# The opening of a gated attention-and-MLP kernel: x halves on two queues, transposes between the first products

## The chip, the cores and the metric

The kernel runs on one core of a Trainium2 chip. Its engines are PE (TensorE, matrix products), DVE (VectorE), ACT (ScalarE), POOL (GpSimd) and SP (SyncE, which here only issues transfers). The metric is the device time of one execution in microseconds. Before the change eight runs gave a median of 148.9 us, from 148.52 to 150.5.

## What is computed

```python
def reference(A_x, A_wqkv, A_w_phi, A_wo, B_x, B_w1, B_w2, gate_w):
    x = A_x                                          # [1, 2048, 512], bf16
    g = sigmoid((x * gate_w).sum(-1, keepdims=True))
    a = A(x, A_wqkv, A_w_phi, A_wo)    # linear attention, 32 heads of 16, softmax feature maps
    b = relu(x @ B_w1) @ B_w2          # 512 -> 1376 -> 512
    return g * a + (1 - g) * b
```

The part that matters here is the start of `b` on the first 512 rows of x, the first x chunk: hidden units are `relu(x @ B_w1)`. The gate's row of 512 weights is put beside `B_w1` as one more column, so that a later product yields the gate's sums as well.

## The kernel before

x is worked on in four chunks of 512 rows. A product on PE contracts over 128 partitions, so x is needed transposed: `XT` holds four feature blocks t of 128 features, each with all rows. Chunks 1 to 3 are transposed by transfers (L172). Chunk 0 is loaded plainly into `XS`, in two halves of 256 rows (L149, events `x00` and `x01`), and transposed by 16 matmuls against an identity (L213, recorded at L217) into PSUM, from where DVE (L227) and ACT (L230) copy it to `XT`.

The order of work is written out by hand. Each engine has a list of operations in program order; an operation names the events that it waits for, and the program turns these into semaphore waits. `free[bank]` names the event after which a PSUM bank may be written again.

The opening goes so:

- ACT's queue issues the load of the gate row (L157). SP's queue issues in this order: the two halves of x (L150), W1 rows of block 0 as a piece of 512 columns and the rest (events `w10a`, `w10`), W1 of blocks 1, 2, 3 (`w11`, `w12`, `w13`; all recorded at L154), then small weights (L164), WV (L166), and the transposed loads (L169, L172).
- PE runs five dummy products (`warm`, L209), the transpose of the gate row (`gatecol`, L203), one dummy product, and 14 of the 16 transposes in four groups. The copies out of PSUM are given to DVE and ACT in turns.
- Then come the slabs (L497). The first eight hidden blocks u of chunk 0 have one PSUM bank each, and slab t adds the product of W1's block (t, u) with `XT` block t into bank u. So a slab is eight products of 512 columns, and four slabs finish eight hidden blocks. Slab 0 is split: four products, the last two transposes, four products. Slabs 1 to 3 follow without a break.
- DVE then does 13 memsets of constants (L519, L521, L524; the last are five, into `EB`), and DVE and ACT apply the ReLU to the eight banks in turns (L241, L239).
- After the slabs PE goes on with two more hidden blocks (`hunit`, L250, recorded at L253), a V tile (`vtile`, L382), projections of the query and key weights (`pre`, L287, eight groups over four banks, copied out by DVE at L292 and ACT at L294), the rest of the hidden columns with the gate column (`rest`, L265), and then the main loop over 16 row tiles.

The banks of the slabs in the order of u are given by:

```python
UB = (3, 4, 5, 0, 6, 7, 2, 1)
```

Of the kernel before, what the change touches and what calls it, by code (L numbers as in the profile page):

```python
# [5 lines left out]
ACT = mybir.ActivationFunctionType  # L6
# [3 lines left out]
BF16 = mybir.dt.bfloat16  # L10
# [47 lines left out]
def bass_gated_mix__linear_kernel_hedgehog__dense_activation_relu__prompt_kernel(  # L58
# [17 lines left out]
    P = 128  # L76
    NT = S // P
    NDT = D // P
# [15 lines left out]
    with ExitStack() as es:  # L94
        E = es.enter_context
        XT = E(nc.sbuf_tensor("XT", [P, NDT, S], BF16))
# [17 lines left out]
        IDN = E(nc.sbuf_tensor("IDN", [P, P], BF16))  # L114
# [4 lines left out]
        GR = E(nc.sbuf_tensor("GR", [NDT, P], BF16))  # L119
# [9 lines left out]
        PS = E(nc.psum_tensor("PS", [P, 8, 512], FP32))  # L129

        XS = OT[:, 0, :].rearrange("p (j d) -> p j d", j=4)
# [7 lines left out]
        p = _Plan(["sp", "pool", "act", "dve", "pe"])  # L139
        free = {b: [] for b in range(8)}  # L140


        xq = x2[0:512, :].rearrange("(p j) d -> p j d", j=4)
# [3 lines left out]
            return oq[:, m, :] if m < 4 else o2[m * P:(m + 1) * P, :]  # L147

        def loadx0(h):  # L149
            p.dma("sp", lambda e: e.dma_start(out=XS[:, 2 * h:2 * h + 2, :], in_=xq[:, 2 * h:2 * h + 2, :]),  # L150
                  f"x0{h}", ev=f"x0{h}")

        def loadw1(t, c0=0, c1=DFF, tag=""):
            p.dma("sp", lambda e: e.dma_start(  # L154
                out=W1[:, t, c0:c1], in_=B_w1[t * P:(t + 1) * P, c0:c1]), f"w1{t}{tag}", ev=f"w1{t}{tag}")

        p.dma("act", lambda e: e.dma_start(out=GR[:, :], in_=gate_w.rearrange("(j p) -> j p", p=P)), "gr", ev="gr")  # L157
        for h in range(2):
            loadx0(h)
        loadw1(0, 0, 4 * P, "a")  # L160
        loadw1(0, 4 * P)
        for t in range(1, NDT):
            loadw1(t)
        p.dma("sp", lambda e: e.dma_start(  # L164
            out=WPS[:, :, :], in_=A_w_phi.rearrange("(g hl) r c -> (hl r) g c", g=NDT)), "wps", ev="wps")
        p.dma("sp", lambda e: e.dma_start(  # L166
            out=WV[:, :, :], in_=A_wqkv[:, 2 * D:3 * D].rearrange("(j p) n -> p j n", p=P)), "wv", ev="wv")
        for i in range(2):
            p.dma("sp", lambda e, i=i: e.dma_start_transpose(  # L169
                out=WQKT[:, 4 * i:4 * i + 4, :], in_=A_wqkv[:, i * D:(i + 1) * D]), f"wqk{i}", ev=f"wqk{i}")  # L170
        for c in range(1, NCH):
            p.dma("sp", lambda e, c=c: e.dma_start_transpose(  # L172
                out=XT[:, :, c * 512:(c + 1) * 512], in_=x2[c * 512:(c + 1) * 512, :]), f"x{c}", ev=f"x{c}")
# [9 lines left out]
            after=["wps"], ev="wd")  # L183
        for gt in range(NDT):
# [4 lines left out]
                after=["wd", "m8"], ev=f"wbd{gt}")  # L189

        p.op("dve", lambda e: e.tensor_tensor(IDN[:, :], ROWI[:, :], COLI[:, :], ALU.is_equal),
             after=["iota0"], ev="idn")
        p.op("dve", lambda e: e.tensor_single_scalar(ROW8[:, :], ROW8[:, :], 4, ALU.arith_shift_right),
             after=["iota"], ev="r8")
# [2 lines left out]
        p.op("dve", lambda e: e.tensor_tensor(M32[:, :], ROW64[:, :], COL16[:, :], ALU.is_equal),  # L197
             after=["r64"], ev="m32")

        def xready(c):  # L200
            return ["xa0", "xa1", "xa2", "xb0", "xb1", "xb3"] if c == 0 else [f"x{c}"]

        def gatecol(bank):  # L203
            gp = PS[:, bank, :].bitcast(BF16)[:, 0:NDT]
            p.op("pe", lambda e: e.transpose(gp, GR[:, :], IDN[0:NDT, 0:NDT]), after=["gr", "idn"], ev="gp")
            p.op("dve", lambda e: e.tensor_copy(W1[:, :, DFF:DFF + 1], gp.unsqueeze(2)), after=["gp"], ev="gw")
            free[bank] = ["gw"]

        def warm(n, cols=512):  # L209
            for _ in range(n):  # L210
                p.op("pe", lambda e: e.matmul(PS[:, 4, 0:cols], ones[:, 0:P], ones[:, 0:cols], start=True, stop=True))

        def xtr(nm, h, dts, bank, evacs):  # L213
            n = 2 * len(dts)
            for i in range(n):
                dt, j = dts[i // 2], 2 * h + i % 2
                p.op("pe", lambda e, i=i, dt=dt, j=j: e.matmul(  # L217
                    PS[:, bank, i * P:(i + 1) * P], XS[:, j, dt * P:(dt + 1) * P], IDN[:, :],
                    start=True, stop=True),
                    after=["idn", f"x0{h}"] + (free[bank] if i == 0 else []), ev=(f"xt{nm}" if i == n - 1 else None))  # L220
            src = PS[:, bank, 0:n * P].rearrange("p (t c) -> p t c", c=256)
            for eng, i0, i1, ev in evacs:
                d = XT[:, dts[i0]:dts[i0] + i1 - i0, h * 256:(h + 1) * 256]
                s = src[:, i0:i1, :]
                if eng == "dve":
                    yield lambda d=d, s=s, ev=ev: p.op(
                        "dve", lambda e: e.tensor_copy(d, s), after=[f"xt{nm}"], ev=ev)  # L227
                else:
                    yield lambda d=d, s=s, ev=ev: p.op(
                        "act", lambda e: e.activation(d, s, ACT.Copy), after=[f"xt{nm}"], ev=ev)  # L230
            free[bank] = [evacs[-1][3]]

        w1all = ["w10a"] + [f"w1{t}" for t in range(NDT)]

# [15 lines left out]
        def hunit(c, kt, eng="act", bank=None):  # L250
            bank = nextbank() if bank is None else bank
            for t in range(NDT):
                p.op("pe", lambda e, t=t: e.matmul(  # L253
                    PS[:, bank, :], W1[:, t, kt * P:(kt + 1) * P], XT[:, t, c * 512:(c + 1) * 512],
                    start=(t == 0), stop=(t == NDT - 1)),
                    after=(xready(c) + w1all + free[bank] if t == 0 else ()),
                    ev=(f"h{c}_{kt}" if t == NDT - 1 else None))
            relu(c, kt, bank, eng)

        def rest(c):  # L260
            bank = nextbank()
            for i in range(4):
                for s in range(NDT):
                    t0 = c * 512 + i * P
                    p.op("pe", lambda e, i=i, s=s, t0=t0: e.matmul(  # L265
                        PS[:, bank, i * P:i * P + NR + 1], XT[:, s, t0:t0 + P], W1[:, s, KU * P:DFF + 1],
                        start=(i == 0 and s == 0), stop=(s == NDT - 1), skip_group_check=True),
                        after=(xready(c) + w1all + ["gw"] + free[bank] if i == 0 and s == 0 else ()),
                        ev=(f"h{c}_r" if i == 3 and s == NDT - 1 else None))
            src = PS[:, bank, :].rearrange("p (i n) -> p i n", i=4)  # L270
            b = c % 2
            p.op("act", lambda e: e.activation(HR[:, b, :, 0:NR], src[:, :, 0:NR], ACT.Relu),
                 after=[f"h{c}_r"] + ([f"hr{c - 2}"] if c >= 2 else []), ev=f"rr{c}")
            p.op("act", lambda e: e.activation(
                EG[:, 4 * c:4 * c + 4].unsqueeze(2), src[:, :, NR:NR + 1], ACT.Exp, scale=-1.0), ev=f"eg{c}")
            free[bank] = [f"eg{c}"]
            p.dma("sp", lambda e: e.dma_start_transpose(
                out=HT[:, KU, c * 512:(c + 1) * 512].rearrange("p (i t) -> p i t", i=4),
                in_=HR[:, b, :, :].rearrange("p i n -> p (i n)")), f"hr{c}", after=[f"rr{c}", f"hz{b}"], ev=f"hr{c}")
# [211 lines left out]


        UB = (3, 4, 5, 0, 6, 7, 2, 1)
        XA = ("xa0", "xa1", "xa2", "xa2")
        XB = ("xb0", "xb1", "xb1", "xb3")

        def slab(t, us=range(8)):  # L497
            for u in us:
                p.op("pe", lambda e, u=u: e.matmul(  # L499
                    PS[:, UB[u], :], W1[:, t, u * P:(u + 1) * P], XT[:, t, 0:512],  # L500
                    start=(t == 0), stop=(t == NDT - 1)),
                    after=["w10a" if t == 0 and u < 4 else f"w1{t}", XA[t], XB[t]] + free[UB[u]],
                    ev=(f"h0_{u}" if t == NDT - 1 else None))

        warm(5)
        gatecol(3)
        warm(1)
        ea = list(xtr("a0", 0, (0, 1), 6, (("dve", 0, 1, "xa0"), ("dve", 1, 2, "xa1"))))
        ec = list(xtr("a1", 0, (2, 3), 7, (("act", 0, 2, "xa2"),)))
        eb = list(xtr("b0", 1, (0,), 2, (("dve", 0, 1, "xb0"),)))  # L510
        ed = list(xtr("b1", 1, (1, 2), 1, (("act", 0, 2, "xb1"),)))
        for fn in (ea[0], eb[0], ea[1], ec[0], ed[0]):
            fn()
        slab(0, range(4))
        for fn in xtr("b2", 1, (3,), 2, (("dve", 0, 1, "xb3"),)):
            fn()
        slab(0, range(4, 8))
        for b in range(VB):
            p.op("dve", lambda e, b=b: e.memset(VS[:, b, :, 64:65], 1.0), ev=f"one{b}")  # L519
        for b in range(2):  # L520
# [2 lines left out]
        for b in range(NB):  # L523
            p.op("dve", lambda e, b=b: e.memset(  # L524
                EB[:, b, 0:3, :].rearrange("p a (g f) -> p (a g) f", f=DH)[:, :, FE:DH], 1.0), ev=f"cst{b}")
        for t in range(1, NDT):
            slab(t)
        for u in range(8):
            relu(0, u, UB[u], ("act", "dve")[u % 2])
        hunit(0, 8)  # L530
# [20 lines left out]
        for m in range(NT):  # L551
# [7 lines left out]
            if m == 3:  # L559
                p.dma("sp", lambda e: e.dma_start(  # L560
                    out=W2[:, 0:KU, :], in_=B_w2[0:KU * P, :].rearrange("(j p) n -> p j n", p=P)), "w2", ev="w20")
                p.dma("sp", lambda e: e.dma_start(out=W2[0:NR, KU, :], in_=B_w2[KU * P:DFF, :]), "w2", ev="w2")
            if m == 5:
                p.dma("sp", lambda e: e.dma_start(
                    out=WO[:, :, :], in_=A_wo.rearrange("(j p) n -> p j n", p=P)), "wo", ev="wo")
# [69 lines left out]
```

## Time and profile before

| | value |
|---|---|
| median of 8 runs | 148.9 us |
| the profiled execution: its time | 148.9 us |
| the profiled execution: its span, first to last instruction | 147.1 us |
| PE busy | 143.7 us (98% of the span) |
| DVE busy | 93.2 us (63%) |
| ACT busy | 72.0 us (49%) |
| POOL busy | 52.1 us (35%) |
| x halves, issue to landing | 2.6 and 3.2 us |
| W1 loads, issue to landing | 3.8 to 6.5 us |

The time of an execution is some 1.8 us longer than its span. Busy time on PE is modelled: a matmul's recorded duration reaches into the next one's, so the pitch of a row of products is read from their starts. "PEld" is the loading of weights, which lies beside the products. A row with "idle before <- releaser" says how long the engine did nothing and which event ended that.

### The profile page before, as it was taken

To read this page: it belongs to the slowest core of one execution; us is meant where nothing else is said; L and a number is where in the kernel's file an instruction comes from. 1 tells how busy PE (TensorE), PEld (TensorE's weight loads), DVE (VectorE), ACT (ScalarE), POOL (GpSimd) and SP (SyncE) were. 2 spreads that over 40 slices of the span, in tenths; PEclk is the share of its full clock that TensorE was granted. 3 is DMA by queue.
4 is the path that set the end of the run, shared out by engine and by line. 5 is a ranking of instruction groups with operands and counts; after the bars stand their busy time and mean duration, and the time that the engine had idled before them with its cause. 6 is when DMAs were issued, how large, how long until landed. Compare 5 with 4: busy or idle time off the path is not lost.

```text
span 147.1 us, 2530 instructions
## 1 busy us (share of the span) xinstructions
PE 143.7 (98%) x978; PEld 73.0 (50%) x978; DVE 93.2 (63%) x157; ACT 72.0 (49%) x123; POOL 52.1 (35%) x62
## 2 busy tenths in 40 slices
PE   7899999999999999999999999999999999999994
PEld 2444744444545645654655555555444444444443
DVE  2527855777788778678698976675444555555342
ACT  3207527887778787877878863012222111111150
POOL 2013000787768678787869820300000000000000
PEclk9999999999999999999999999999999999999999
DMA  4999994033349967334643430454333323222213
GB/s 149 255 304 183 245 185 107 0 71 71 76 79 301 206 165 105 71 71 107 55 95 71 107 71 15 92 110 109 76 89 82 78 72 76 71 71 74 71 40 107
DMA packets 44644, 16.11 MB, mean 110 GB/s; under 512 B 39288, under 2 KB 43992, under 8 KB 44632
## 3 DMA queue, kind: packets, MB, share of 16 engines
q1 hardware_dynamic: 44480, 15.92, 48.3%
q8 instruction: 8, 0.13, 0.4%
q10 hardware_dynamic: 152, 0.03, 0.1%
q14 instruction: 4, 0.03, 0.1%
HBM read 4.41 MB, written 2.10 MB: 44 GB/s over the span
## 4 chain that ended last, share of the span: by engine, by line
PE 93%; DMA 4%; SPq 1%; DVE 1%; issue 0%
PE PS L461 25%; PE PS L253 19%; PE PS L307 18%; PE PS L470 9%; PE PS L382 9%; PE PS L499 4%; DMA W<-in_B_w_dram 4%; PE PS L436 3%; PE PS L404 3%; PE PS L265 2%; PE PS L287 1%; DVE WQK L484 1%; SPq L154 1%; SPq L150 1%
## 5 line engine op out<-in xcount | busy, mean ns | idle before, releaser
L461 PE MATMUL PS<-W,HT 128*128 128x512 bf16 (+4 forms) x187 | 40.6, 366 | 0.0
L326 ACT ACTIVATE EB<-PS 128x480 bf16<-128x480 f32 (+1 forms) x44 | 30.1, 756 | 15.9 <-PE PS L307 15.9
L350 POOL TENSOR_TENSOR EB<-EB,SC 128x1024 bf16<-128x1024 bf16 x15 | 29.0, 1930 | 24.3 <-DVE SC L348 24.3
L475 ACT ACTIVATE TFA<-PS,GT 128x512 bf16<-128x512 f32 x16 | 11.0, 687 | 42.7 <-PE PS L470 36.6
L253 PE MATMUL PS<-XT,W 128*128 128x512 bf16 x128 | 30.7, 379 | 0.0
L307 PE MATMUL PS<-WQK,XT 128*128 128x480 bf16 x128 | 28.5, 366 | 0.0
L484 DVE SCALAR_TENSOR_TENSOR WQK<-PS,OMG,TFA 128x512 bf16<-128x512 f32 (+2 forms) x17 | 12.2, 719 | 23.6 <-ACT TFA L475 22.4
L346 DVE TENSOR_REDUCE ZB<-EB 128x64 f32<-128x1024 bf16 x15 | 18.3, 1220 | 13.9 <-ACT EB L326 13.9
L461 PEld LDWEIGHTS PS<-W,HT 128*128 128x128 bf16 (+1 forms) x187 | 17.0, 98 | 17.4
L239 ACT ACTIVATE HT<-PS 128x512 bf16<-128x512 f32 x35 | 20.3, 614 | 7.9 <-PE PS L499 6.0
L307 PEld LDWEIGHTS PS<-WQK,XT 128*128 128x128 bf16 x128 | 12.5, 98 | 13.8
L361 DVE TENSOR_REDUCE ZB<-EB 128x64 f32<-128x1024 bf16 x16 | 18.6, 1164 | 0.0
L253 PEld LDWEIGHTS PS<-XT,W 128*128 128x128 bf16 x128 | 12.0, 98 | 13.2
L370 POOL TENSOR_TENSOR EB<-EB,SC 128x512 bf16<-128x512 bf16 x16 | 16.9, 1059 | 1.2
L382 PE MATMUL PS<-WV,XT 128*128 128x512 bf16 x64 | 16.2, 378 | 0.0
L470 PE MATMUL PS<-WO,OT 128*128 128x512 bf16 x64 | 16.1, 378 | 0.0
L446 DVE TENSOR_TENSOR WQK<-PS,RDEN 128x512 bf16<-128x512 f32 x16 | 11.1, 692 | 0.6
L470 PEld LDWEIGHTS PS<-WO,OT 128*128 128x128 bf16 x64 | 6.1, 97 | 7.2
L348 DVE RECIPROCAL SC<-ZB 128x64 f32<-128x64 f32 x16 | 8.8, 553 | 0.5
L499 PE MATMUL PS<-XT,W 128*128 128x512 bf16 x32 | 7.5, 380 | 0.6 <-DMA W<-in_B_w_dram 0.4
L382 PEld LDWEIGHTS PS<-WV,XT 128*128 128x128 bf16 x64 | 5.5, 97 | 4.9
L392 ACT ACTIVATE VS<-PS 128x512 bf16<-128x512 f32 x13 | 7.9, 609 | 0.0
(55 smaller groups left out, 87.5 us busy)
## 6 DMA issues: line engine op xcount, KB each, us to landing
out_dram<-WQK SPq DMA_DIRECT2D x15, 128.0 KB, 1.7
W<-in_B_w_dram SPq DMA_DIRECT2D x1, 1280.0 KB, 6.7
W<-in_B_w_dram SPq DMA_DIRECT2D x3, 344.0 KB, 5.9
OT<-in_A_x_dram SPq DMA_DIRECT2D x2, 256.0 KB, 2.9
WV<-in_A_wqkv_dram SPq DMA_DIRECT2D x1, 512.0 KB, 7.2
WO<-in_A_wo_dram SPq DMA_DIRECT2D x1, 512.0 KB, 4.0
PHQ<-EB SPq DMA_TRANSPOSE x16, 2.7
OT<-WQK SPq DMA_TRANSPOSE x16, 2.4
```

Of the source, the lines that this page charges most:

```text
L239: p.op("act", lambda e: e.activation(dst, src, ACT.Relu), after=[f"h{c}_{kt}"], ev=ev)
L253: p.op("pe", lambda e, t=t: e.matmul(PS[:, bank, :], W1[:, t, kt * P:(kt + 1) * P], XT[:, t, c * 512:(c + 1) * 512], start=(t == 0), stop= ...
L307: p.op("pe", lambda e, dt=dt, which=which: e.matmul(PS[:, which, 0:DE], XT[:, dt, m * P:(m + 1) * P], WQK[:, which, dt * DE:(dt + 1) * DE] ...
L326: p.op("act", lambda e: e.activation(dst, s_, ACT.Exp, scale=scale), after=[f"qk{m}"] + busy, ev=ev)
L346: p.op("dve", lambda e: e.tensor_reduce(zk, ek, AX.X, ALU.add), after=[emk, f"cst{b}"], ev=f"zk{m}")
L350: p.op("pool" if m < NT - 1 else "dve", lambda e: e.tensor_tensor(EB[:, b, 3, :].rearrange("p (g f) -> p g f", f=DH), EB[:, b, 2, :].rearr ...
L361: p.op("dve", lambda e: e.tensor_reduce(ZB[:, b, 0:64].rearrange("p (h s) -> p h s", s=2), bass.AP(tensor=EB, offset=base, ap=[[EBS, P], [ ...
L370: p.op("pool", lambda e: e.tensor_tensor(EB[:, b, 0, :].rearrange("p (h s f) -> p h s f", h=H, s=2)[:, :, 1, :], EB[:, b, 1, :].rearrange( ...
L382: p.op("pe", lambda e, dt=dt: e.matmul(PS[:, bank, :], XT[:, dt, m * P:(m + 1) * P], WV[:, dt, :], start=(dt == 0), stop=(dt == NDT - 1)), ...
L461: p.op("pe", lambda e, kt=kt, M=M: e.matmul(PS[:, bank, 0:n], HT[0:M, kt, m * P:(m + 1) * P], W2[0:M, kt, cs], start=(kt == 0), stop=(kt = ...
L470: p.op("pe", lambda e, t=t: e.matmul(PS[:, bank, :], OT[:, t, m * P:(m + 1) * P], WO[:, t, :], start=(t == 0), stop=(t == NDT - 1)), after ...
L484: p.op("dve", lambda e: e.scalar_tensor_tensor(out=OSB[:, ob, cs], in0=PS[:, bank, 0:n], scalar=OMG[:, m:m + 1], in1=TFA[:, m % 2, cs], op ...
```

## The change

Four things are changed, all in the opening.

1. The second half of the x chunk is issued on ACT's queue in place of SP's, ahead of the gate row's load, which moves behind it.
2. A transpose group is now one feature block, copied out by one instruction: block 0 in two halves of two transposes each (DVE copies one, ACT the other), blocks 1, 2 and 3 as groups of four over both halves (DVE, ACT, DVE).
3. Only block 0 is transposed ahead of the first slab products. The other 12 transposes come after the first four products of slab 0. Then come unit 4 of slab 0, units 0 to 4 of slab 1, the gate row's transpose, and units 7, 5, 6 of slabs 0 and 1 by pairs; their banks are those that the transposes used.
4. The gate row's transpose writes into the last columns of bank 2 and waits for that bank; one dummy product takes its old place. On DVE the copy of the gate column comes after the x copies and stands ahead of the 13 memsets.

```diff
         def loadx0(h):
-            p.dma("sp", lambda e: e.dma_start(out=XS[:, 2 * h:2 * h + 2, :], in_=xq[:, 2 * h:2 * h + 2, :]),
+            p.dma(("sp", "act")[h], lambda e: e.dma_start(out=XS[:, 2 * h:2 * h + 2, :], in_=xq[:, 2 * h:2 * h + 2, :]),
                   f"x0{h}", ev=f"x0{h}")
...
-        p.dma("act", lambda e: e.dma_start(out=GR[:, :], in_=gate_w.rearrange("(j p) -> j p", p=P)), "gr", ev="gr")
         for h in range(2):
             loadx0(h)
+        p.dma("act", lambda e: e.dma_start(out=GR[:, :], in_=gate_w.rearrange("(j p) -> j p", p=P)), "gr", ev="gr")
...
+        X0 = (["x0a", "x0b"], ["x1ab"], ["x2ab"], ["x3ab"])
...
-            gp = PS[:, bank, :].bitcast(BF16)[:, 0:NDT]
-            p.op("pe", lambda e: e.transpose(gp, GR[:, :], IDN[0:NDT, 0:NDT]), after=["gr", "idn"], ev="gp")
+            gp = PS[:, bank, :].bitcast(BF16)[:, 1020 - NDT:1020]
+            p.op("pe", lambda e: e.transpose(gp, GR[:, :], IDN[0:NDT, 0:NDT]), after=["gr", "idn"] + free[bank], ev="gp")
...
+        def xtr(dt, hs, bank, eng):
+            nm = f"x{dt}" + "".join("ab"[h] for h in hs)
+            js = [2 * h + i for h in hs for i in range(2)]
+            for i, j in enumerate(js):
+                p.op("pe", lambda e, i=i, j=j: e.matmul(
+                    PS[:, bank, i * P:(i + 1) * P], XS[:, j, dt * P:(dt + 1) * P], IDN[:, :],
+                    start=True, stop=True),
+                    after=["idn"] + [f"x0{h}" for h in hs] + (free[bank] if i == 0 else []),
+                    ev=(f"t{nm}" if i == len(js) - 1 else None))
+            src = PS[:, bank, 0:len(js) * P]
+            dst = XT[:, dt, js[0] * P:(js[-1] + 1) * P]
...
+            free[bank] = [nm]
...
-        warm(5)
-        gatecol(3)
+        warm(6)
+        xtr(0, (0,), 6, "dve")
+        xtr(0, (1,), 7, "act")
         warm(1)
-        ea = list(xtr("a0", 0, (0, 1), 6, (("dve", 0, 1, "xa0"), ("dve", 1, 2, "xa1"))))
-        ec = list(xtr("a1", 0, (2, 3), 7, (("act", 0, 2, "xa2"),)))
-        eb = list(xtr("b0", 1, (0,), 2, (("dve", 0, 1, "xb0"),)))
-        ed = list(xtr("b1", 1, (1, 2), 1, (("act", 0, 2, "xb1"),)))
-        for fn in (ea[0], eb[0], ea[1], ec[0], ed[0]):
-            fn()
         slab(0, range(4))
-        for fn in xtr("b2", 1, (3,), 2, (("dve", 0, 1, "xb3"),)):
-            fn()
-        slab(0, range(4, 8))
+        xtr(1, (0, 1), 2, "dve")
+        xtr(2, (0, 1), 1, "act")
+        xtr(3, (0, 1), 7, "dve")
+        slab(0, (4,))
+        slab(1, range(5))
+        gatecol(2)
...
-        for t in range(1, NDT):
-            slab(t)
+        for u in (7, 5, 6):
+            slab(0, (u,))
+            slab(1, (u,))
+        slab(2)
+        slab(3)
```

More of the change, by code (lines that the diff above doesn't have):

```diff
@@ L198, in bass_gated_mix__linear_kernel_hedgehog__dense_activation_relu__prompt_kernel @@
              after=["r64"], ev="m32")
+        X0 = (["x0a", "x0b"], ["x1ab"], ["x2ab"], ["x3ab"])
         def xready(c):
-            return ["xa0", "xa1", "xa2", "xb0", "xb1", "xb3"] if c == 0 else [f"x{c}"]
+            return [e for t in range(NDT) for e in X0[t]] if c == 0 else [f"x{c}"]
         def gatecol(bank):
-            gp = PS[:, bank, :].bitcast(BF16)[:, 0:NDT]
-            p.op("pe", lambda e: e.transpose(gp, GR[:, :], IDN[0:NDT, 0:NDT]), after=["gr", "idn"], ev="gp")
+            gp = PS[:, bank, :].bitcast(BF16)[:, 1020 - NDT:1020]
+            p.op("pe", lambda e: e.transpose(gp, GR[:, :], IDN[0:NDT, 0:NDT]), after=["gr", "idn"] + free[bank], ev="gp")
             p.op("dve", lambda e: e.tensor_copy(W1[:, :, DFF:DFF + 1], gp.unsqueeze(2)), after=["gp"], ev="gw")
@@ L211, in warm @@
                 p.op("pe", lambda e: e.matmul(PS[:, 4, 0:cols], ones[:, 0:P], ones[:, 0:cols], start=True, stop=True))
[L213 to L217, printed above, removed]
+        def xtr(dt, hs, bank, eng):
[3 more added lines that the diff above has]
+                p.op("pe", lambda e, i=i, j=j: e.matmul(
                     PS[:, bank, i * P:(i + 1) * P], XS[:, j, dt * P:(dt + 1) * P], IDN[:, :],
                     start=True, stop=True),
[L220 to L231, printed above, removed]
+                    after=["idn"] + [f"x0{h}" for h in hs] + (free[bank] if i == 0 else []),
+                    ev=(f"t{nm}" if i == len(js) - 1 else None))
+            src = PS[:, bank, 0:len(js) * P]
+            dst = XT[:, dt, js[0] * P:(js[-1] + 1) * P]
+            if eng == "dve":
+                p.op("dve", lambda e: e.tensor_copy(dst, src), after=[f"t{nm}"], ev=nm)
+            else:
+                p.op("act", lambda e: e.activation(dst, src, ACT.Copy), after=[f"t{nm}"], ev=nm)
+            free[bank] = [nm]
         w1all = ["w10a"] + [f"w1{t}" for t in range(NDT)]
@@ L493, in bass_gated_mix__linear_kernel_hedgehog__dense_activation_relu__prompt_kernel @@
         UB = (3, 4, 5, 0, 6, 7, 2, 1)
-        XA = ("xa0", "xa1", "xa2", "xa2")
-        XB = ("xb0", "xb1", "xb1", "xb3")
         def slab(t, us=range(8)):
@@ L501, in slab @@
                     start=(t == 0), stop=(t == NDT - 1)),
-                    after=["w10a" if t == 0 and u < 4 else f"w1{t}", XA[t], XB[t]] + free[UB[u]],
+                    after=["w10a" if t == 0 and u < 4 else f"w1{t}", *X0[t]] + free[UB[u]],
                     ev=(f"h0_{u}" if t == NDT - 1 else None))
-        warm(5)
-        gatecol(3)
+        warm(6)
+        xtr(0, (0,), 6, "dve")
+        xtr(0, (1,), 7, "act")
         warm(1)
-        ea = list(xtr("a0", 0, (0, 1), 6, (("dve", 0, 1, "xa0"), ("dve", 1, 2, "xa1"))))
-        ec = list(xtr("a1", 0, (2, 3), 7, (("act", 0, 2, "xa2"),)))
-        eb = list(xtr("b0", 1, (0,), 2, (("dve", 0, 1, "xb0"),)))
-        ed = list(xtr("b1", 1, (1, 2), 1, (("act", 0, 2, "xb1"),)))
-        for fn in (ea[0], eb[0], ea[1], ec[0], ed[0]):
-            fn()
-        slab(0, range(4))
-        for fn in xtr("b2", 1, (3,), 2, (("dve", 0, 1, "xb3"),)):
-            fn()
-        slab(0, range(4, 8))
+        slab(0, range(4))
+        xtr(1, (0, 1), 2, "dve")
[4 more added lines that the diff above has]
+        gatecol(2)
         for b in range(VB):
```

## The prediction

> **What bounds the kernel now.** I read the page first: PE is busy 143.7 of 147.1 us, and the chain that ended last is 93% PE. So the kernel is a PE stream, and a change in its first microseconds counts only by how much it moves the moment from which PE never waits again. Next I read the chain of waits in order of time for the first 15 us (columns: start, length, what):
>
> ```profile
> 1.66 0.42 SPq L154
> ...
> 2.13 0.43 SPq L154
> ...
> 2.60 5.20 DMA W<-in_B_w_dram
> 7.80 0.05 issue
> 7.85 5.35 PE PS L499 x24
> 13.20 1.73 PE PS L253 x8
> ```
>
> That moment is 7.85 us. It is set by a transfer: the third W1 load (rows of feature block 1, event w11), issued at 2.60 and landed at 7.80. From there the 24 slab products of blocks 1 to 3 and all that follows run without a hole. The 24 products give PE's pitch: (5.35 - 0.38) / 23 = 0.216 us each, the last one's own duration being 0.38.
>
> Third, the timeline of the opening (start, length, engine, line, operation, count, idle time before and who ended it):
>
> ```profile
> 3.51 1.55 PE L217 MATMUL PS<-IDN,OT 128*128 128x128 bf16 x14
> 4.61 1.09 ACT L230 ACTIVATE XT<-PS 128x512 bf16<-128x512 f32 x2 [2.00 <-PE PS L217]
> 4.87 0.76 DVE L227 CAST XT<-PS 128x256 bf16<-128x256 f32 x2 [0.27 <-PE PS L217]
> 5.49 1.04 PE L499 MATMUL PS<-XT,W 128*128 128x512 bf16 x4 [0.43 <-DMA W<-in_B_w_dram]
> 6.37 0.28 PE L217 MATMUL PS<-IDN,OT 128*128 128x128 bf16 x2
> 6.48 6.72 PE L499 MATMUL PS<-XT,W 128*128 128x512 bf16 x28
> ...
> 7.84 4.86 PEld L499 LDWEIGHTS PS<-XT,W 128*128 128x128 bf16 x24 [0.57 <-DMA W<-in_B_w_dram]
> 8.04 0.22 DVE L524 MEMSET EB<- 128x192 bf16 x1 [0.60 <-issue]
> 8.85 0.22 DVE L524 MEMSET EB<- 128x192 bf16 x1 [0.59 <-issue]
> ...
> 11.95 2.48 DVE L241 TENSOR_SCALAR HT<-PS 128x512 bf16<-128x512 f32 x4 [0.43 <-PE PS L499]
> ...
> 16.44 2.42 DVE L292 CAST WQK<-PS 128x480 bf16<-128x480 f32 x4
> ...
> 17.23 1.07 PE L287 MATMUL PS<-Wbd,PHQ 128*128 128x120 bf16 x16
> ```
>
> To see: 14 transposes run before the first slab product, which starts at 5.49 when the 128 KB W1 piece lands (issued 1.66, 3.8 us to landing). All eight products of block 0 are done by about 7.6, so they lie under the wait for w11. The two transposes at 6.37 take 0.11 together, 0.055 each. On DVE each EB memset takes a place of 0.81 us (8.04 to 8.85), mostly idle, and they end just before the first ReLU.
>
> Last, the windows of a quarter microsecond, for the share of the 16 DMA engines and GB/s (the last two columns):
>
> ```profile
> 2.25:2.50 0.25, 0.25 (x2) 0.00 (x0) 0.03 (x1) 0.25 (x1) 0.00 (x0) 1.00 0.99 377
> ...
> 3.50:3.75 0.25, 0.25 (x4) 0.23 (x3) 0.00 (x0) 0.00 (x0) 0.00 (x0) 1.00 0.77 238
> ...
> 6.75:7.00 0.25, 0.25 (x2) 0.00 (x0) 0.25 (x1) 0.00 (x0) 0.00 (x0) 1.00 0.88 242
> ```
>
> The engines are working from 2.0 us on, at 0.75 to 1.1 of their time. The loads wait for the transfer engines, not for the queue that issues them.
>
> **What the Trainium skill says.** "DMA: Bandwidth & Descriptors", section "Issuing engines are not separate DMA queues", says that DMAs issued from several engines run on the same 16 DMA engines and that issuing on two saves only sequencer time. The trace agrees on the size of that time, 0.42 us an issue, and on the engines being taken; it has no two large loads on two queues at once. The same page, "Queues, rings and completion order", says that an engine alternates between the queues that have work. That gives no more bandwidth, only another order; no row of before shows it. "TensorE: Matmul & The Clock Gate", Part 1, says that PE runs at half rate until it was busy for a window of about 3.4 us. The trace agrees: five transposes from 3.51 span 0.74 with 0.31 for one, so 0.107 a step, against 0.055 at 6.37.
>
> **The change part by part.** All sums are against the profiled execution: span 147.1, time 148.9, which equals the median of the eight runs; 1.8 us lie outside the span.
>
> *The second half of x on ACT's queue.* One issue of 0.42 leaves SP ahead of the W1 loads, so w11 is issued at about 2.14 and not 2.60; all later SP loads go 0.46 earlier too. ACT's queue issues the x half (about 0.4), then the gate row, then loads its table (1.28), done near 3.1; its first eviction comes after 4.8. But the bytes ahead of w11 are the same: 2 x 256 + 128 + 216 + 344 KB. Bounds on w11's landing: 0 earlier (engines full) to 0.46 earlier (all issue-bound). I take 0.1, because the share is above 0.75 all the way; the dips near 3.5 leave a little. So w11 lands at 7.7 and slab 1 starts at S = 7.75. The later transposed loads come earlier and nobody waits for them now (PE has no gap at L287).
>
> *Ten transposes moved behind the first four products.* Ahead of the first product there are now 4. It starts no earlier for that: it waits for the W1 piece (5.49 now), and for the second x half: issued at 1.19 with 3.2 us to landing, 4.4, plus two transposes and the eviction, about 0.9, gives 5.3. So 5.3 to 5.5. Then 4 products (0.86), 12 transposes at 0.055 (0.66), 1 product (0.22) end at about 7.2. The eviction of block 1 by DVE (512 wide, 0.69 by the L241 row's first element) is ready at about 7.3. Both are before S, so this costs nothing while w11 lands after 7.3. If w11 came earlier, 7.35 would be the start.
>
> *Three products of block 0 moved behind slab 1.* Units 5, 6, 7 need the banks in which the transposes stand, and are put after the first five products of slab 1. PE runs its products in the order of the program (in the trace of before without exception), so they cannot fill the wait for w11 as they do now. Behind w11 stand now 27 products in place of 24: 3 x 0.216 = +0.65. This is the main term. The hole ahead of S becomes about 0.5 us, and no work is left for it.
>
> *The gate transpose moved behind slab 1's fifth product.* Its matmul goes from the dead time at 3.00 (next one at 3.11) into the stream: +0.11. Unit 6 uses its bank and waits for the DVE copy (0.18); four products (0.86) lie between, so no stall. The gate row's load is issued later on ACT, near 1.2; in before it took 2.3 us from issue to PE's start (0.74 to 3.00), so it is there long before S.
>
> *Who is queued behind the gate copy.* On DVE it now stands ahead of 13 memsets, and it waits for slab 1. Five products (1.08), the matmul's 0.22 to the copy and the copy's 0.18 put its end at S + 1.5. Eight small memsets take 0.36 (7.08 to 7.44 before), five EB memsets 0.81 each: DVE is free for its first ReLU at S + 5.9 = 13.65, where it was at 11.95. Then 4 + 1 ReLUs and one V eviction at a pitch of (2.48 - 0.69) / 3 = 0.60, and the first WQK eviction (0.65): done at S + 5.9 + 3.6 + 0.65 = S + 10.15 = 17.9. PE wants that bank for the fifth projection group at 17.23 + 0.66 = 17.9. So the backlog is just about hidden; the next one (pitch 0.59) and the wake-up cost some hundredths. Bounds: 0 to 0.5 (if the memsets' 0.6 idle also follows the last one). I take +0.1.
>
> *Sum.* -0.1 + 0.65 + 0.11 + 0.1 = +0.76: the first L253 product goes from 13.04 in the timeline (7.85 + 24 x 0.216) to 13.8, the span to 147.9, the time to 149.7. PE has no waits after that which could take the delay back.
>
> **The rivals.**
> (A) The issue time reaches w11 in full: it lands at 7.34, S = 7.4, and the sum is -0.45 + 0.65 + 0.11 + 0.1 = +0.4: 149.3. For it: the share of 0.77 near 3.5. Against: shares near 1 elsewhere, and a W1 piece of 344 KB that takes over 1.2 us at 280 GB/s, so the queue is full behind it.
> (B) PE is still at half rate when the slab begins. Warm-up ends at 0.77 + 6 x 0.43 = 3.35, and until 5.4 there are only four transposes and one dummy, so the busy window that released the clock at about 4.6 now has a hole of a microsecond or more. If release comes one window of 3.4 us later, at 8.0 (an estimate from the page named above and the observed 4.6), then 4 products at 0.43 end at 7.2, 7 transposes at 0.107 reach 8.0, and the rest ends at 8.5: S = 8.5, +0.75 more, 150.5. For it: idle PE where there was none. Against: the page does not say how full the window must be.
> (C) The other side: two queues make the opening transfers faster, not only sooner issued. If the second x half landed with the first, 2.6 us after issue, at 3.4, and all behind it moved up by 1.1, the first product starts at 4.4. The stream from there to L253 is 32 x 0.216 + 12 x 0.055 + 0.11 + about 0.15 of waiting for block 1 = 7.8, so 12.2 instead of 13.04: -0.8 + 0.1 = -0.7, 148.2. It decides from w11 landing about 0.85 us earlier, with the first product at 5.1 or before. Against: 320 to 377 GB/s while x moves, the highest of the opening, so no room for twice as much.
> That the moved transposes do not help at all is inside the forecast.
>
> **How the numbers follow.** Forecast 0.50 (149.7; own range 149.3 to 150.0), A 0.22 (149.3), B 0.20 (150.5), C 0.08 (148.2 to 149). About 0.5% (0.74 us) is what a measurement of this kernel can tell from no change, so the line is at 149.6. Slower: 0.32 of the forecast's half, and all of B, 0.53. Same: the rest of the forecast, A, and half of C, 0.43. Faster: 0.04. The range of 149.0 to 150.5 leaves out most of C and the upper end of B.
>
> **What would show it.** In the profile of the changed kernel: SPq's first W1 issue near 1.2; the chain again passing through a W1 transfer that lands at 7.5 to 7.8; a PE idle of about half a microsecond ended by it; then 27 products and one 4-wide transpose before L253 starts near 13.8; DVE's first ReLU (L240 there) near 13.7. Rival B shows as slab products at 0.43 spacing. The prediction is wrong if w11 lands before 7.0, if DVE's memsets go faster once they stand later, or if L253 starts at 13.1 or before.

## The result, and the profile after

The changed kernel took 150.51 us in the median of 22 runs (149.02 to 151.25), the kernel before 148.86 us (59 runs, 148.18 to 150.72). The ratio of the comparison is 1.0092, with a 95% interval from 1.0073 to 1.0111: slower by about 1%. Ratios leave out executions more than 1.5% above the fastest of the same kernel, while medians and ranges are of all executions. The 22 runs form two groups with nothing in between, 8 from 149.02 to 149.44 and 14 from 150.38 to 151.25; the median falls into the upper group, and the quotient of the medians is 1.011. Of the kernel before, 57 of the 59 runs lie below 149.6, and the other two at 150.50 and 150.72, where the upper group is. The profiled execution of the changed kernel took 151.17 us with a span of 149.5, so it belongs to the upper group.

Its chain of waits in order of time, until the end of the slabs (start, length, what):

```profile
0.74 3.46 DMA OT<-in_A_x_dram
4.20 0.14 issue
4.34 0.60 PE PS L219 x4
4.93 0.02 issue
4.96 0.39 ACT XT L229
5.35 0.14 issue
5.49 1.87 PE PS L495 x4
7.35 1.28 PE PS L219 x12
8.63 2.01 PE PS L495 x6
...
10.75 4.85 PE PS L495 x22
```

The W1 transfer that set the start of slab 1 before is no longer in the chain. PE itself is, from 5.49 us on, with the same work taking much longer. The four first products take 1.87 where before four took 1.04. The first product starts at 5.49 in both; before, the first W1 piece released it, and now ACT's copy of the second half of block 0. The first product after the slabs is that of L252 (L253 before). These are the rows of before and after in the timelines:

```profile
13.04 1.89 PE L253 MATMUL PS<-XT,W 128*128 128x512 bf16 x8
```

```profile
15.44 1.89 PE L252 MATMUL PS<-XT,W 128*128 128x512 bf16 x8
```

That is +2.4 us, and the spans differ by as much (149.5 - 147.1). So none of the difference arises after that point.

PE's rows in the timeline of the changed kernel, from 2.5 to 12 us (the last row is cut off there):

```profile
2.00 1.49 PE L213 MATMUL PS<-const-bfloat16-1.0 128*128 128x512 bf16 x3
4.34 0.58 PE L219 MATMUL PS<-IDN,OT 128*128 128x128 bf16 x4 [0.84 <-DMA OT<-in_A_x_dram]
4.72 0.63 PE L213 MATMUL PS<-const-bfloat16-1.0 128*128 128x512 bf16 x1
5.49 1.87 PE L495 MATMUL PS<-XT,W 128*128 128x512 bf16 x4
7.14 1.49 PE L219 MATMUL PS<-IDN,OT 128*128 128x128 bf16 x12
8.43 2.22 PE L495 MATMUL PS<-XT,W 128*128 128x512 bf16 x6
10.57 0.17 PE L207 MATMUL PS<-IDN,GR 4*128 4x4 bf16 x1
10.68 1.68 PE L495 MATMUL PS<-XT,W 128*128 128x512 bf16 x7
```

From 5.49 to 7.14 four products pass, 0.41 each, and from 7.14 to 8.43 twelve transposes, 0.107 each. That is half the rate of before (0.216 and 0.055). The last row has seven products in 1.68, (1.68 - 0.38) / 6 = 0.217 each: by then the rate is full. The starts of the single products show the change at about 9.9: they are at 9.28, 9.71, 10.04 and 10.26. Ahead of all this PE stands still from about 3.3 to 4.3 us, after the last dummy, because the first x half now lands at 4.20 and not at 3.35. This stretch without work is called the long hole below; a shorter one lies ahead of the first product. The slow products with the hole ahead of them are rival B of the prediction.

The text calls the rate of PE its clock, as the prediction does. No column shows this clock: the one for the granted clock says 1.00 throughout, in the changed kernel too, as in this window (the last three columns are granted clock, busy share of the DMA engines and GB/s; the kernel before first, then the changed one):

```profile
6.00:8.00 2.00, 1.83 (x10) 0.57 (x9) 0.76 (x9) 0.00 (x0) 0.00 (x0) 1.00 0.95 293
```

```profile
6.00:8.00 2.00, 2.00 (x13) 1.18 (x11) 0.18 (x1) 0.00 (x0) 0.00 (x0) 1.00 1.00 339
```

Half and full rate are read from the pitch alone: the dummies at the start of every profile follow each other at 0.43, and the same shape later at 0.216.

### The profile page after: what moved, and what is told of

It is laid out like the page before. It is cut to its first block, busy times and chain, and to the rows that moved or that the text cites. A ratio compares the mean times of both kernels' runs of the same rounds, so it can differ in the third digit from the quotient of the medians.

```text
span 149.5 us, 2531 instructions
## 1 busy us (share of the span) xinstructions
PE 145.7 (98%) x979; PEld 73.9 (49%) x979; DVE 93.2 (62%) x156; ACT 71.9 (48%) x123; POOL 52.1 (35%) x62
## 4 chain that ended last, share of the span: by engine, by line
PE 95%; DMA 2%; DVE 1%; ACT 0%; issue 0%
PE PS L460 25%; PE PS L252 18%; PE PS L306 17%; PE PS L469 9%; PE PS L381 9%; PE PS L495 6%; PE PS L435 3%; PE PS L403 3%; DMA OT<-in_A_x_dram 2%; PE PS L264 2%; PE PS L219 1%; PE PS L286 1%; DVE WQK L483 1%; ACT XT L229 0%; PE PS L207 0%
## 5 line engine op out<-in xcount | busy, mean ns | idle before, releaser
L252 PE MATMUL PS<-XT,W 128*128 128x512 bf16 x128 | 30.7, 379 | 0.0
L252 PEld LDWEIGHTS PS<-XT,W 128*128 128x128 bf16 x128 | 12.0, 98 | 13.2
L495 PE MATMUL PS<-XT,W 128*128 128x512 bf16 x32 | 9.0, 438 | 0.1
```

The costliest lines, as they stand in the source:

```text
L252: p.op("pe", lambda e, t=t: e.matmul(PS[:, bank, :], W1[:, t, kt * P:(kt + 1) * P], XT[:, t, c * 512:(c + 1) * 512], start=(t == 0), stop= ...
L495: p.op("pe", lambda e, u=u: e.matmul(PS[:, UB[u], :], W1[:, t, u * P:(u + 1) * P], XT[:, t, 0:512], start=(t == 0), stop=(t == NDT - 1)), ...
```

## The experiments

Two theories were set against each other. Theory 1: the hole in PE's opening keeps its clock at half rate, in most executions until long after the products have begun. Theory 2: the new order of products and copies costs the time by itself. "Filling" a hole means putting dummy products into it. All runs were taken beside runs of the kernel before (median 148.91 in the first set of experiments, 148.94 in the second).

### The changed kernel with the holes filled

```diff
-        warm(6)
+        warm(8)
         xtr(0, (0,), 6, "dve")
         xtr(0, (1,), 7, "act")
-        warm(1)
+        warm(2)
```

> The changed kernel with 8 dummy products in place of 6 ahead of the first transposes and 2 in place of 1 behind them, so that PE works through from 0.8 to about 5.5 us. Theory 1 (the holes in PE's opening keep its clock at half rate until about 10 us in most executions, and cost 1.4 us): all slab products at a pitch of 0.216, the first L252 product at about 13.3 to 13.5, and all runs near 149.1, the lower of the two groups that the changed kernel's runs form; nothing at 150.4 to 151.2. Theory 2 (the new order of the products and copies costs the time, the pitch only goes along with it): the two groups stay, median near 150.5.

Measured: 149.16 us in the median (148.98 to 150.0, 22 runs), ratio 1.0032 (1.0016 to 1.0047). No run lies above 150.0, where 14 of 22 did. Three dummy products more make the kernel 1.35 us faster in the median. PE's rows of its timeline over the same stretch:

```profile
2.01 2.34 PE L213 MATMUL PS<-const-bfloat16-1.0 128*128 128x512 bf16 x5
4.40 0.38 PE L219 MATMUL PS<-IDN,OT 128*128 128x128 bf16 x4
4.62 0.60 PE L213 MATMUL PS<-const-bfloat16-1.0 128*128 128x512 bf16 x2
5.35 1.02 PE L495 MATMUL PS<-XT,W 128*128 128x512 bf16 x4
6.21 0.83 PE L219 MATMUL PS<-IDN,OT 128*128 128x128 bf16 x12
6.88 0.38 PE L495 MATMUL PS<-XT,W 128*128 128x512 bf16 x1
7.47 1.24 PE L495 MATMUL PS<-XT,W 128*128 128x512 bf16 x5 [0.21 <-DVE XT L227]
8.64 0.17 PE L207 MATMUL PS<-IDN,GR 4*128 4x4 bf16 x1
8.75 3.63 PE L495 MATMUL PS<-XT,W 128*128 128x512 bf16 x15
```

The order is that of the changed kernel, and everything from 4.40 on runs at full clock. Slab 1 starts at 7.47, released by DVE's copy of block 1 out of PSUM, and its first L252 product is at 13.51. So Theory 1 holds for the large part of the loss: the group above 150.2 goes when the holes are filled, with the order unchanged. What is left of it in this pair of profiles is 13.51 - 13.04 = 0.47 us.

### The kernel before with a hole

```diff
-        warm(5)
+        warm(3)
         gatecol(3)
-        warm(1)
```

> The kernel before with 3 dummy products in place of 5 and without the one behind the gate transpose: PE is idle from about 2.1 to 3.4 us, and order, queues and copies are those of before. Theory 1: the clock is released late in many or most runs, slab products at 0.43 in the profile, median 149.5 to 150.5 or two groups with an upper one over 150. Theory 2: no change, 148.9 within 0.3.

Measured: 149.46 us (149.03 to 150.45, 22 runs), ratio 1.0037 (1.0019 to 1.0056). Four runs are above 150.2; of the 69 runs of the kernel before beside this set three were. PE's rows of its timeline:

```profile
3.42 1.68 PE L217 MATMUL PS<-IDN,OT 128*128 128x128 bf16 x14 [1.09 <-DMA OT<-in_A_x_dram]
5.28 1.86 PE L499 MATMUL PS<-XT,W 128*128 128x512 bf16 x4 [0.18 <-DVE XT L227]
6.93 0.42 PE L217 MATMUL PS<-IDN,OT 128*128 128x128 bf16 x2
7.15 5.09 PE L499 MATMUL PS<-XT,W 128*128 128x512 bf16 x21
```

The four products take 1.86, as in the changed kernel: half rate, with the order of before. The cost is smaller (0.55 us in the median). In this profile that is because the rate was full from about 8 us, and because slab 1 of the kernel before had to wait for w11 until 7.85 in any case: here w11 lands at 6.74 and slab 1 starts at about 8.40 (the first L253 product, at 13.58, less 24 x 0.216). The median is just below the expected 149.5 to 150.5, and a hole of over a microsecond did not make an upper group of more than four runs here.

### The second queue alone

```diff
-            p.dma("sp", lambda e: e.dma_start(out=XS[:, 2 * h:2 * h + 2, :], in_=xq[:, 2 * h:2 * h + 2, :]),
+            p.dma(("sp", "act")[h], lambda e: e.dma_start(out=XS[:, 2 * h:2 * h + 2, :], in_=xq[:, 2 * h:2 * h + 2, :]),
```

> The kernel before with the second x half on ACT's queue, behind the gate row; all W1 loads are issued about 0.46 us earlier, PE's order and dummies are those of before. If the transfers depend on the issue (the prediction's case A): w11 lands at 7.0 to 7.4, and the time falls by the wait for it, about 0.25, to 148.6. If the DMA engines set it, as the prediction took: w11 lands at 7.7, time 148.8 to 148.9. Theory 1 expects no late clock here, since PE has no new hole.

Measured: 150.26 us (148.76 to 152.44, 22 runs), ratio 1.0057 (1.003 to 1.0085). This was a miss: neither 148.6 nor 148.9, and 12 of 22 runs lie above 150.2. From the chain of its profile (an execution of 151.02):

```profile
0.74 0.56 ACTq L157
1.30 0.03 issue
1.33 3.89 DMA OT<-in_A_x_dram
```

and from PE's rows of the timeline:

```profile
5.27 0.82 PE L217 MATMUL PS<-IDN,OT 128*128 128x128 bf16 x6 [0.70 <-DMA OT<-in_A_x_dram]
6.27 1.87 PE L499 MATMUL PS<-XT,W 128*128 128x512 bf16 x4 [0.18 <-DVE XT L227]
```

The second x half lands at 5.22, later than with one queue (4.44). Behind the gate row it is issued at 1.33. The first W1 piece, issued on SP at 1.20, lands at 4.25, where before it landed at 5.45, behind both x halves. That the two loads take from each other fits this, but is not shown by itself. So PE had a new hole after all, ahead of its last transposes, and again the four products take 1.87. The statement "no new hole" in the expectation was wrong, so this run says nothing on the worth of the second queue at full clock. It shows that the second queue alone can open a hole.

### The order alone, at full clock

```diff
-            p.dma(("sp", "act")[h], lambda e: e.dma_start(out=XS[...
+            p.dma("sp", lambda e: e.dma_start(out=XS[...
...
         warm(6)
         xtr(0, (0,), 6, "dve")
+        warm(2)
         xtr(0, (1,), 7, "act")
-        warm(1)
+        warm(2)
```

> The changed kernel with both x halves on SP's queue as before, and the holes of PE filled with dummies (6, 2 between the halves of block 0, 2 behind). The order alone, at full clock. The prediction's sum: w11 lands at 7.8, 27 products and the gate transpose behind it (+0.65 +0.11), DVE's backlog +0.1: 149.7. If the order's cost was over-estimated: 149.3 or less. If the order and not the clock makes the upper group: 150.5.

Measured: 149.70 us (149.18 to 150.46, 16 runs), ratio 1.0057 (1.0037 to 1.0077). The chain of its profile, an execution of 149.34:

```profile
2.60 4.78 DMA W<-in_B_w_dram
7.38 0.05 issue
7.42 1.25 PE PS L495 x5
```

The median is what the sum of the prediction says for the order at full clock, and the mechanism is the one it names: slab 1 waits for w11. But in this execution w11 lands at 7.38, not at 7.8, and the execution is 0.36 below the median. The landing differs between executions, and the agreement of the sum with the median is partly luck.

Beside the filled changed kernel this run gives a worth of the second queue: with the same order and the holes filled, two queues are 0.54 us faster in the medians (149.16 against 149.70) and 0.40 in the means. The dummies stand a little differently in the two, so this is not the queue entirely alone.

### Which of the two holes

Two runs with the changed kernel, each filling one hole: 8 dummies ahead of the transposes and 1 behind, or 6 ahead and 2 behind.

```diff
-        warm(6)
+        warm(8)
```

> The changed kernel with 8 dummies in place of 6 ahead of the transposes, 1 behind them as it has: PE works through from 0.8 to 4.9 us and keeps the hole of half a microsecond before the first product. Theory 1 with the long hole (3.3 to 4.3) as its cause: as the filled one, 149.1 to 149.3 with few runs above 150. If any hole in the opening holds the clock: two groups again.

```diff
-        warm(1)
+        warm(2)
```

> The changed kernel with 2 dummies in place of 1 behind the transposes and 6 ahead as it has: the hole from 3.3 to 4.3 us stays, that before the first product is filled. If the long hole is the cause: two groups as in the changed kernel, median over 150. If the second hole is: 149.2.

Measured: with the first hole filled 149.48 us (148.98 to 150.07, 22 runs), ratio 1.0042 (1.0024 to 1.0059), none above 150.2. With only the second filled 150.52 us (148.99 to 151.31, 22 runs), ratio 1.0074 (1.0048 to 1.0101), and 12 of 22 above 150.2, as two groups. So in the changed kernel the long hole makes the upper group; with the short one left, the median is 0.3 above that of the filled form (149.16) and above the 149.1 to 149.3 expected. The profile of the first of these runs (149.9) shows half rate too:

```profile
4.14 0.63 PE L219 MATMUL PS<-IDN,OT 128*128 128x128 bf16 x4
4.57 0.63 PE L213 MATMUL PS<-const-bfloat16-1.0 128*128 128x512 bf16 x1
5.34 1.70 PE L495 MATMUL PS<-XT,W 128*128 128x512 bf16 x4
6.87 0.83 PE L219 MATMUL PS<-IDN,OT 128*128 128x128 bf16 x12
```

The four products take from 5.34 to 6.87, and only the transposes behind them are at full rate (12 in 0.67), although PE worked without a break from 0.77 to about 5.0. The profile of the second run fell in its lower group (149.18). PE's rows there:

```profile
4.12 0.59 PE L219 MATMUL PS<-IDN,OT 128*128 128x128 bf16 x4 [0.63 <-DMA OT<-in_A_x_dram]
4.50 0.96 PE L213 MATMUL PS<-const-bfloat16-1.0 128*128 128x512 bf16 x2
5.30 1.03 PE L495 MATMUL PS<-XT,W 128*128 128x512 bf16 x4
```

The hole is there, 0.2 us shorter than in the profile of the changed kernel (the first x half landed at 3.98 here, and at 4.20 there), and the four products still take 1.03. With the same program some executions have the clock in time and others do not; whether these 0.2 us decide it, no run tells.

### A version that uses the waits, with two queues and with one

The transposes of blocks 1 and 2 and the gate's go into the time in which block 0 is copied out, and units 6 and 7 of slab 0 ahead of slab 1.

```diff
-        warm(6)
+        warm(8)
         xtr(0, (0,), 6, "dve")
         xtr(0, (1,), 7, "act")
-        warm(1)
-        slab(0, range(4))
+        gatecol(0)
         xtr(1, (0, 1), 2, "dve")
         xtr(2, (0, 1), 1, "act")
+        slab(0, range(4))
         xtr(3, (0, 1), 7, "dve")
-        slab(0, (4,))
+        slab(0, (4, 6, 7))
         slab(1, range(5))
-        gatecol(2)
...
-        for u in (7, 5, 6):
-            slab(0, (u,))
-            slab(1, (u,))
+        slab(0, (5,))
+        slab(1, (5, 6, 7))
```

> A version from what the runs showed: the changed kernel with 8 dummies at the start, and the time in which block 0 is copied out of PSUM used by the gate transpose and the transposes of blocks 1 and 2; only block 3 is transposed behind the first four products, and three of the last four products of slab 0 come ahead of slab 1. Theory 1: PE works through to the first product, so one group of runs at full clock; the first product at about 5.35, slab 1 at about 7.2 with 25 products behind it, the first L252 product at 12.6 where the kernel before has 13.04 and the filled changed kernel 13.51: 148.3 to 148.5. If block 1's copy is not what holds slab 1 but the order of W1's landing: 148.9 or more.

> The better order with both x halves on SP's queue, 6 dummies, 2 between the halves of block 0. It tells what the second queue is worth at full clock. With w11 at 7.4 to 7.8, slab 1 starts there and L252 at 12.8 to 13.3: 148.7 to 149.2, some 0.4 to 0.6 above the version with two queues. If the second queue is worth nothing: the same as that version, 148.4.

Measured: with two queues 148.50 us (147.99 to 148.9, 22 runs), ratio 0.9968 (0.9952 to 0.9983): faster than the kernel before. With one queue (6 dummies, and 2 between the halves) 148.65 us (148.2 to 149.59, 22 runs), ratio 0.9983 (0.9963 to 1.0004): no difference that can be told. From the chain of the first:

```profile
2.15 5.17 DMA W<-in_B_w_dram
7.32 0.05 issue
7.37 5.57 PE PS L495 x25
```

Now w11 is again what the stream waits for, at 7.32, and 25 products stand behind it. With them L252 begins at 7.37 + 25 x 0.216 = 12.77 (the timeline has 12.78), and 13.04 - 12.78 = 0.26 is gained in this pair of profiles. The expectation had 12.6 for that product and was met in the time. It had tied a start that W1's landing sets to 148.9 or more, and that was wrong. For the one-queue version 0.4 to 0.6 more than with two was expected; the medians differ by 0.15 and the means by 0.33. It was at half clock until about 6.4 us in its profile, so this isn't the worth of the queue alone either.

## Why the prediction was right or wrong

The direction was right, and the size was not: 149.7 was forecast, 150.51 measured, at the edge of the range (150.5). The forecast's own branch had full clock. The upper group, 14 of 22 runs, is where rival B lies, which had a chance of 0.20, and the profile from this group shows rival B's mechanism. That "slower" came true is partly luck: with the holes filled the same order and queues cost 0.25 us, less than the 0.74 that the prediction takes as the least that can be told from no change.

The medians of three runs split the loss. The new order alone costs 149.70 - 148.91 = +0.79, where the forecast's terms for it are 0.65 + 0.11 + 0.1 = 0.86. The second queue gives 149.16 - 149.70 = -0.54, forecast -0.1. The holes give 150.51 - 149.16 = +1.35, forecast nothing. In the ratios, which do not jump with the median, these are about +0.85, -0.37 and +0.9. So the order was priced about right, the queue's gain was underrated, and the clock was left out.

**The step that failed** is "Ten transposes moved behind the first four products", in its line "4 products (0.86), 12 transposes at 0.055 (0.66)". These were priced at full clock. The profile has 1.65 and 1.29 for them. Between the changed kernel and its filled form, from the first product to the first L252, the terms are: four products +0.79, twelve transposes +0.62, the next product and the wait behind it -0.17, five slab-1 products and the gate +0.55, a start later by 0.14. Together that is 1.93, as much as 15.44 - 13.51. What stands behind it is a term that the step "The second half of x on ACT's queue" put at nothing without a reason: it asks what the second queue does to w11 and never to the first x half, which it delayed from 3.35 to 4.20. That put the long hole behind the dummies. Rival B had the mechanism and its place, but let the clock be released at 8.0 and added 0.75; in the profile half rate lasted to nearly 10 us.

**The steps at full clock**, read from the filled form, where 0.47 came of a forecast 0.76:

- The start of slab 1: forecast 7.75, set by w11; it was 7.47, set by block 1's copy. W1's middle load of five, w11, was issued at about 2.14 and took 4.9 in the changed kernel and 5.0 in the filled one, so it landed at 7.0 and 7.2. The step "Bounds on w11's landing: 0 earlier (engines full) to 0.46 earlier", of which 0.1 was taken, was off. But the 7.80 of before was itself a late one: with one queue the profiles have 6.7, 7.2, 7.4 and 7.8, with two 6.8 to 7.3. How much of this is the earlier issue and how much the variation isn't settled by these profiles. The reason given for 0.1, a share "above 0.75 all the way", was misread. The windows of before have lower ones ahead of w11's landing, such as this:

```profile
5.00:5.25 0.25, 0.06 (x2) 0.00 (x0) 0.25 (x2) 0.25 (x2) 0.00 (x0) 1.00 0.56 218
```

And a share near 1 did not mean that the engines move all they can: from 6 to 8 us the kernel before moved 293 GB/s at 0.95 and the changed one 339 at 1.00, as the two windows in the section on the result show.
- The floor of 7.35 for the start, named in that step as what comes next, was right within 0.12. It is what bound the filled form.
- Three products moved behind slab 1: +0.65, as forecast.
- The gate transpose: forecast 0.11. From 7.47 to 8.75 there are five products (1.08) and the gate: 0.20.
- DVE's backlog: forecast +0.1, measured 0. In the changed kernel the first ReLU of DVE does come late, at 15.00 among the last memsets, where S + 5.9 with this profile's S of 8.85 gives 14.75. These are rows of its timeline:

```profile
15.00 0.88 DVE L240 TENSOR_SCALAR HT<-PS 128x512 bf16<-128x512 f32 x1 [0.45 <-PE PS L495]
15.15 0.22 DVE L518 MEMSET EB<- 128x192 bf16 x1
...
19.63 1.07 PE L286 MATMUL PS<-Wbd,PHQ 128*128 128x120 bf16 x16
```

The second row of projections starts at 19.63, against 17.23 before: +2.40, the same as at L252. So nothing was added in between.

So the four terms at full clock give -0.38 (7.47 instead of 7.85) + 0.65 + 0.20 + 0 = 0.47, as measured between the profiles. In the medians the filled form is 0.25 above the kernel before. The chances of the prediction are a hundredth off their own parts: 0.32 and 0.20 make 0.52 for slower, and the rest 0.44 for same.

**Rival A** (149.3) is near what the changed kernel's lower group shows (149.02 to 149.44), though not by its mechanism alone: in the profiles of the new order with two queues and the full rate, the copy of block 1 was the bound, and not w11. **Rival C** did not happen for the x halves: the first landed at 4.20, the second at about 4.0, so the two shared what one had. That agrees with the Trainium skill, "DMA: Bandwidth & Descriptors", section "Issuing engines are not separate DMA queues". The W1 loads behind them are another matter. The section says that issuing on two engines saves only the time of the issue, which was 0.46 us here. But the last two W1 loads landed 1.76 to 1.95 us after w11 in the six profiles with two queues and 2.25 to 2.55 after it in the four with one, and from 5.25 to 6.75 us the DMA engines moved 339 to 376 GB/s with two and 285 to 316 with one, at a busy share of 0.93 to 1.05 in all. So these loads were faster, and not only sooner issued, though all of them are on SP's queue in both cases. Here the measurement decides, and it shows more than the saved time of the issue; the cause stays open. Rival C's first product at 4.4 did not come of it: it started at 5.49.

The first x half paid for the sharing: its landing went from 3.35 to 4.20, and this is what opened the hole. The prediction had seen the hole, from the end of the dummies, but gave no weight to the fact that the dummies before had been enough to last until the data came.

What stays open: what decides in one execution whether the clock is released in time. The Trainium skill, "TensorE: Matmul & The Clock Gate", Part 1, says that the window of about 3.4 us in which activity is measured runs free of the kernel's start. Two groups with the same program, and full rate reached in the profiles anywhere from 3.7 us (the order alone, holes filled) to 10.3 (the second queue alone), agree with that. In the first of these PE had its first product at 0.77, so 2.9 us of work were enough, less than one whole window; in the run with only the first hole filled 4.2 us of unbroken work were not. So "busy for a window of about 3.4 us", as the prediction has it, is not a count of time from PE's first product. No run here set the phase of the window, so it is not shown.

## What to carry to other kernels

Where dummy work keeps PE busy ahead of the first data, as here, it has to last until the data is there: when a change moves the landing of the first data, the dummies have to be counted anew. Here a microsecond of idle PE cost 1.36 us in the median (150.52 with the second hole filled, 149.16 with both), more than the 0.79 that the new order cost. Work that is ready belongs into the waits themselves, here the transposes into the time of the first copies; behind the wait each product costs its full 0.216 us. And a landing time read from one profile says little: that of w11 ran from 6.7 to 7.8 us over four profiles with the same loads in the same order. A step resting on it needs both ends.

## What the runs showed of the hardware that was not expected

- Two loads of 256 KB issued at the same moment on two queues landed at 4.02 and 4.20 us in the changed kernel; on one queue, one behind the other, they landed at 3.35 and 4.44 in the kernel before. Over all profiles the half that PE needs first landed at 3.35 to 3.39 with one queue and at 3.95 to 4.27 with two (issued together), the last half at 3.99 to 4.52 and at 4.12 to 4.27. So the loss of the first one is sure, the gain of the last one is within the spread.
- The W1 loads behind the x halves moved faster with two queues: 339 to 376 GB/s against 285 to 316 from 5.25 to 6.75 us, at the same busy share of the DMA engines. The share doesn't tell whether they move all they can.
- A load on the second queue that was issued 0.13 us after a smaller one on the first landed late: issued at 1.33, it took 3.89 us, where on one queue it took 2.8 to 3.3. This is one profile.
- An idle PE of about one microsecond, from about 3.3 us on, in an opening that was otherwise busy from 0.8 us on, put 12 of 22 executions into a group that is 1.4 us slower (the changed kernel with the second hole filled). With a hole of 1.1 us in the order of before, from about 2.3 us on, only 4 of 22 lay above 150.2.
